# Attention outputs as half-width products, two groups in one run, in a kernel of gated linear attention and two mixtures of experts

## The chip, the cores and the metric

The kernel runs on one core of a Trainium2 chip. The metric is the device time of one execution in microseconds (us). The instruction streams that matter here are TensorE (PE; its weight loads are listed apart as PEld), VectorE (DVE), ScalarE (ACT), GpSimd (POOL) and SyncE (SP), whose queue issues nearly all DMAs of the part of the program that is changed. Each engine works through its own instructions in the order in which the program has them, and waits on semaphores where an instruction needs something of another engine or of a DMA.

## The reference

Three layers follow one another. The first is a linear attention with a decaying state, for 2 batches, 8 heads, 768 tokens and 48 features a head; the outputs of the 8 heads side by side are the 384 features of 1536 tokens. The second is a dense mixture of 4 experts (384 to 1024 to 384), the third a mixture of 8 experts of which each token takes two.

```python
for t in range(S):                                   # attention, per batch and head
    state = alpha[:, :, t, :, None] * state + np.einsum('bhd,bhe->bhde', k[:, :, t], v[:, :, t])
    y[:, :, t] = np.einsum('bhd,bhde->bhe', q[:, :, t], state)

p = domain_probs / (domain_probs.sum(-1, keepdims=True) + 1e-09)      # first mixture
for e in range(E):
    out += p[:, e:e + 1] * (np.maximum(x @ w1[e], 0.0) @ w2[e])

noisy_logits = x @ w_gate + np.log1p(np.exp(x @ w_noise)) * noise     # second mixture, top 2 of 8
```

## The kernel before, in words

**Units.** The 1536 tokens go through the attention in seven units u0 to u6 of 128, 256, 256, 128, 256, 256 and 256 tokens. Heads are worked in pairs: pair p holds head 2p on partitions 0 to 47 and head 2p+1 on partitions 64 to 111. A group is two blocks of (pair, 128-token chunk): a 128-token unit has two groups (pairs 0 and 1, then 2 and 3), a 256-token unit four (one pair with its two chunks each).

**Steps of a group.** `reversed_`, `decays`, `keys`, `queries` transpose alpha, k and q on TensorE (L301) and scale them on VectorE; `scores` (L374) makes the products of keys and queries, with the two heads of a pair on the two halves of TensorE's rows; `keys_back` (L359) transposes the scaled keys, ScalarE copies them to `Kn` (L361); `states` (L397) adds the chunk to the state `St` (VectorE, L404 to L413). `outputs` (L417) makes y: for each block one product of the state with the queries (L427, "inter"), and for each head of the pair one product of v with the masked scores (L430, "intra"), all into the same 96 rows of PSUM. For L430 the v of a head is padded with 48 zero columns, so that both heads of the pair have 96 columns and add into the same rows.

**x, the input of the first mixture.** The mixture's first layer contracts 384 features as three slices `kd` of 128 rows. Pairs 0 to 2 are rows 0 to 95 of the slices; the 96 features of pair 3 are cut in three and fill rows 96 to 127 of each. ScalarE rounds y into `xh` (L451), VectorE writes the rest into `xl` (L455); for pair 3 these are three pieces of 32 rows. For u0 the pieces go to `x32` as plain copies (L446, L448; the profile names the tile `acc`, in whose space it lies). The weights `w1` of experts 0 to 3 are loaded in the same row order, in two DMAs for each quarter (96 and 32 rows, L126).

**What sets the order.** `plan` puts the steps of each group into numbered steps by two tables, NEAR (first three groups) and FAR (the others: `outputs` at +9 in even and +7 in odd groups, a new group every 3 steps). `drive` interleaves them with the first mixture's expert 0, which runs in phases of tokens: 128 (u0), 256 (u1), 384 (u2 and u3), and 256 three times (u4 to u6). A phase starts when the last unit of its tokens is done. In a phase `hidden` makes the first layer (L548 for the first 128 tokens; L552 to L554 otherwise: three products for each `kd`), `product` the second (L572 to L574). What `outputs` leaves to VectorE (`low`) is put into `later` and is issued at the end of its step. DMAs stand in SP's queue in the order in which the program comes to them: the first ones by the list in L649, the others where a step calls `load_unit`. `busy(n)` issues products of ones whose result nothing reads.

**Start.** Before u0 there is `busy(7)` (L197, L200); then alpha, k, q of u0 are transposed as they land.

## Time and profile before

| | us |
|---|---|
| median of 3 runs (lowest, highest) | 743.19 (743.07, 743.55) |
| the profiled execution, its own time | 742.35 |
| span of its trace | 740.4 |
| TensorE busy in the span | 730.3 |
| VectorE, ScalarE, GpSimd busy | 355.6, 244.8, 164.2 |

The profiled execution is 0.84 us below the median; 1.95 us of its time lie outside the span. The attention ends near 166 us of the span; everything that the diff touches lies before that, except the split of the weight loads of experts 1 to 3. TensorE is busy in nearly the whole span, so the view to start from is the one of engines by stretch, and then the places where TensorE stands still or is short of work: the first 40 us.

### The profile page before, as it was taken

The numbers are of one execution on the slowest core, as the hardware profiler recorded it, in microseconds if no ns is written. First come the engines' busy times: TensorE is split into PE (matmuls) and PEld (weight loads), VectorE is DVE, ScalarE is ACT, GpSimd is POOL, SyncE is SP. The second block draws the span as 40 slices with busy tenths as digits, with TensorE's granted clock in tenths as the row PEclk, the third lists the DMA queues.
The fourth block names the chain that finished last, engine by engine and source line by source line (L and its number), as shares of the span: only waits on it lengthen the run. The fifth ranks groups of instructions, "written<-read, shape, count | busy, mean of one in ns | idle before, by whom it ended". The sixth has DMA issues, their size and how long they took to land.

```text
span 740.4 us, 11896 instructions
## 1 busy us (share of the span) xinstructions
PE 730.3 (99%) x4598; PEld 695.7 (94%) x4598; DVE 355.6 (48%) x863; ACT 244.8 (33%) x483; POOL 164.2 (22%) x180
## 2 busy tenths in 40 slices
PE   8999999999999999999999999999999999999996
PEld 6999999999898998989899999999999999999996
DVE  6887667743312222221222525557854464664651
ACT  2543223224302122120413412424544354454340
POOL 3610000005300022000324100012251624524331
PEclk9999999999999999999999999999999999999999
DMA  9985220002700022000123100012754555555620
GB/s 193 204 192 96 40 48 1 1 1 87 196 22 1 0 86 64 23 0 1 44 86 125 35 33 12 22 44 79 246 175 138 180 163 162 188 182 157 192 64 32
DMA packets 98381, 66.96 MB, mean 90 GB/s; under 512 B 57961, under 2 KB 94884, under 8 KB 98320
## 3 DMA queue, kind: packets, MB, share of 16 engines
q1 hardware_dynamic: 93296, 52.02, 26.2%
q0 software_dynamic: 5024, 14.13, 6.0%
q8 instruction: 38, 0.62, 0.3%
q14 instruction: 23, 0.19, 0.1%
HBM read 56.69 MB, written 9.82 MB: 90 GB/s over the span
## 4 chain that ended last, share of the span: by engine, by line
PE 93%; DVE 5%; ACT 1%; issue 0%; POOL 0%; POOLq 0%; DVEq 0%
PE g L552 13%; PE g L553 13%; PE g L554 13%; PE g L572 11%; PE g L573 10%; PE g L574 10%; PE g L1090 3%; PE g L1091 3%; PE g L1092 3%; PE g L430 3%; PE tr L301 2%; PE sc L374 1%; PE tr L1024 1%; PE g L427 1%; PE sc L749 1%; PE sc L397 1%
## 5 line engine op out<-in xcount | busy, mean ns | idle before, releaser
L557 ACT ACTIVATE hh<-g 128x384 fp32r<-128x384 f32 (+8 forms) x200 | 96.8, 484 | 265.2 <-PE g L554 263.6
L561 DVE SCALAR_TENSOR_TENSOR hl<-g,hh 128x384 fp32r<-128x384 f32 (+8 forms) x200 | 109.4, 549 | 144.7 <-ACT hh L557 141.9
L572 PE MATMUL g<-w2h,hl 128*128 128x384 f32 x464 | 161.4, 348 | 0.0
L573 PE MATMUL g<-w2l,hh 128*128 128x384 f32 x464 | 156.1, 336 | 0.0
L574 PE MATMUL g<-w2h,hh 128*128 128x384 f32 x464 | 156.1, 336 | 0.0
L552 PE MATMUL g<-xh,w1l 128*128 128x512 f32 (+2 forms) x360 | 125.8, 349 | 0.0
L554 PE MATMUL g<-xh,w1h 128*128 128x512 f32 (+2 forms) x360 | 123.2, 342 | 0.0
L553 PE MATMUL g<-xl,w1h 128*128 128x512 f32 (+2 forms) x360 | 123.2, 342 | 0.0
L572 PEld LDWEIGHTS g<-w2h,hl 128*128 128x128 f32 x464 | 87.3, 188 | 0.5
L573 PEld LDWEIGHTS g<-w2l,hh 128*128 128x128 f32 x464 | 87.5, 188 | 0.3
L150 POOL TENSOR_TENSOR w1l<-raw,w1h 128x768 fp32r<-128x768 f32 x16 | 29.4, 1852 | 260.8 <-ACT w1h L149 260.8
L574 PEld LDWEIGHTS g<-w2h,hh 128*128 128x128 f32 x464 | 87.2, 188 | 0.0
L605 DVE SCALAR_TENSOR_TENSOR acc<-g,prob,acc 128x384 f32<-128x384 f32 x36 | 22.2, 618 | 116.6 <-PE g L574 116.6
L554 PEld LDWEIGHTS g<-xh,w1h 128*128 128x128 f32 x360 | 67.6, 188 | 5.8
L552 PE MATMUL g<-xth,w1l 128*128 128x256 f32 (+6 forms) x216 | 73.0, 338 | 0.0
L553 PEld LDWEIGHTS g<-xl,w1h 128*128 128x128 f32 x360 | 67.8, 188 | 5.5
L552 PEld LDWEIGHTS g<-xh,w1l 128*128 128x128 f32 x360 | 67.7, 188 | 5.4
L553 PE MATMUL g<-xtl,w1h 128*128 128x256 f32 (+6 forms) x216 | 71.0, 329 | 0.0
L554 PE MATMUL g<-xth,w1h 128*128 128x256 f32 (+6 forms) x216 | 71.0, 329 | 0.0
L149 ACT ACTIVATE w2h<-raw 128x768 fp32r<-128x768 f32 x44 | 37.0, 845 | 36.1 <-issue 23.0
L1042 POOL DMA_INDIRECT out_dram<-yo,si_c x26 | 26.1, 1004 | 87.6 <-DVE yo L1041 81.1
L1090 PE MATMUL g<-hh,w2l 128*128 128x432 f32 (+4 forms) x120 | 43.3, 361 | 0.0
(211 smaller groups left out, 1036.2 us busy)
## 6 DMA issues: line engine op xcount, KB each, us to landing
raw<-in_moe_w_dram SPq DMA_DIRECT2D x76, 384.0 KB, 3.3
raw<-in_moe_w_dram SPq DMA_DIRECT2D x16, 288.0 KB, 3.8
x_a<-in_alpha_dram SPq DMA_DIRECT2D x24, 96.0 KB, 2.8
out_dram<-zero SPq DMA_DIRECT2D x1, 2304.0 KB, 10.9
x2d<-acc SPq DMA_DIRECT2D x12, 192.0 KB, 1.9
x_k<-in_k_dram SPq DMA_DIRECT2D x22, 96.0 KB, 3.0
x_q<-in_q_dram SPq DMA_DIRECT2D x22, 96.0 KB, 2.8
v<-in_v_dram SPq DMA_DIRECT2D x10, 192.0 KB, 3.2
```

The costliest lines, as they stand in the source:

```text
L149: nc.scalar.activation(hi, r, AF.Copy)
L150: (nc.gpsimd if e < E1 or own else nc.vector).tensor_sub(lo, r, hi.bitcast(F32))
L552: nc.tensor.matmul(t[:, :n], wl, hx[:, kd, t0:t0 + n], start=(kd == 0), stop=False)
L553: nc.tensor.matmul(t[:, :n], wh, lx[:, kd, t0:t0 + n], start=False, stop=False)
L554: nc.tensor.matmul(t[:, :n], wh, hx[:, kd, t0:t0 + n], start=False, stop=(kd == KD - 1))
L557: nc.scalar.activation(hh[:, :n], t[:, :n], AF.Relu)
L561: nc.vector.scalar_tensor_tensor(hl[:, :n], t[:, :n], 0.0, hh.bitcast(F32)[:, :n], op0=OP.max, op1=OP.subtract)
L572: nc.tensor.matmul(t[:m, :DM], hl[:, o:o + m], wh, start=(f == 0), stop=False)
L573: nc.tensor.matmul(t[:m, :DM], hh[:, o:o + m], wl, start=False, stop=False)
L574: nc.tensor.matmul(t[:m, :DM], hh[:, o:o + m], wh, start=False, stop=(f == KF - 1))
L1042: nc.gpsimd.indirect_dma_start(out=parts_of_out[s], out_offset=bass.IndirectOffsetOnAxis(ap=SLOT[e * SB + s][2][:n, e * SB + s:e * SB + s ...
L1090: nc.tensor.matmul(t[:, :n], wl, hh[:, :n], start=(f == 0), stop=False)
```

## The change

Parts of it, in the order of the program:

- The weights `w1` of experts 0 to 3 come in four DMAs a quarter (48, 16, 48, 16 rows) instead of two: 64 instead of 32 issues, 8 of the 32 new ones in the list of the start.
- `busy(5)` instead of `busy(7)`.
- v is held with 16 zero columns behind the 48 of each head, the state with 128 columns instead of 96.
- Groups come with pairs 2 and 3 first, then 0 and 1, and the loads of u0 and u1 follow that.
- The intra products become halves: 64 columns of weights each, head 2p into rows 0 to 63 of PSUM, head 2p+1 into rows 64 to 127, on the two halves of TensorE's columns (`halves`, L427 of the changed kernel). The inter product (L458 there) has 128 columns.
- `outputs` does nothing for even groups and both groups at the odd one: first the four inter products, then the eight halves, in one PSUM bank. In u1 to u6 this makes 11 runs out of 22.
- u0 has a function of its own (`first_outputs`): ten halves instead of eight products; ScalarE then copies six pieces of 32 rows and two of 48, VectorE two of 48.
- Of x, heads 2p lie on rows 0 to 47 and 2p+1 on 64 to 111 of slice p; the features of pair 3 fill rows 48 to 63 and 112 to 127. Pair 3 of u1 to u6 is written to a tile `tail` by ScalarE and VectorE, and six DMAs from SBUF to SBUF (16 rows each, both `xh` and `xl`) put it there; they are issued by SP, at the end of the step, after VectorE's part. In a 256-token unit ScalarE and VectorE have four pieces each (two of 128 rows, two of 48) instead of six (three of 96 rows, three of 32).

```diff
@@ -121,12 +121,16 @@
                 r = wpool.tile([P, KD * FG * P], F32, tag="raw", name="raw", bufs=4)
             if t == 1:
                 n = FG * P
-                parts = ((0, P),) if e >= E1 else ((0, 2 * D), (2 * D, P))
-                for p0, p1 in parts:
-                    nc.sync.dma_start(
-                        r.rearrange("p (c f) -> p c f", c=KD)[p0:p1],
-                        w[KD * p0:KD * p1, g * n:(g + 1) * n].rearrange("(c p) f -> p c f", c=KD),
-                    )
+                to = r.rearrange("p (c f) -> p c f", c=KD)
+                cols = slice(g * n, (g + 1) * n)
+                if e >= E1:
+                    nc.sync.dma_start(to, w[:, cols].rearrange("(c p) f -> p c f", c=KD))
+                else:
+                    for j in range(2):
+                        o = (2 * KD + j) * D
+                        nc.sync.dma_start(to[64 * j:64 * j + D],
+                                          w[:2 * D * KD, cols].rearrange("(c j q) f -> j q c f", c=KD, j=2)[j])
+                        nc.sync.dma_start(to[64 * j + D:64 * j + 64], w[o:o + D, cols].rearrange("(c q) f -> q c f", c=KD))
             else:
                 nc.sync.dma_start(
                     r.rearrange("p (c f) -> p c f", c=FG),
@@ -197,7 +201,7 @@
-    busy(7)
+    busy(5)
@@ -228,7 +232,7 @@
-    V = [apool.tile([P, BM, H, 2, D], F32, name=f"v{i}") for i in range(2)]
+    V = [apool.tile([P, BM, H, 64], F32, name=f"v{i}") for i in range(2)]
@@ -257,7 +261,7 @@
-    St = apool.tile([P, HP, BM + 1, 2 * D], F32, name="S")
+    St = apool.tile([P, HP, BM + 1, P], F32, name="S")
@@ -267,18 +271,18 @@
-    xh = xpool.tile([P, KD, N], F32R, name="xh")
-    xl = xpool.tile([P, KD, N], F32R, name="xl")
+    xx = xpool.tile([P, 2, KD, N], F32R, name="xx")
+    xh, xl = xx[:, 0], xx[:, 1]
@@ -286,7 +290,7 @@
-        groups = [[(g * BM // UB + i // UB, i % UB) for i in range(BM)] for g in range(HP * UB // BM)]
+        groups = [[((g * BM // UB + i // UB + 2) % HP, i % UB) for i in range(BM)] for g in range(HP * UB // BM)]
@@ -395,64 +399,92 @@
...
+        def halves(t, todo, opened):
+            v = V[u % 2].rearrange("x c h d -> x c (h d)")
+            for i, (M, p, c, by) in enumerate(todo):
+                for j in range(2):
+                    o = 64 * (2 * p + j) - by
+                    nc.tensor.matmul(t[64 * j:64 * j + 64, at(i)], v[:, c, o:o + 64], M[j], start=not opened and i == 0,
+                                     stop=i == len(todo) - 1)
+
+        def first_outputs(g):
+            t = ps("g", 4)
+            todo = [([st[g, j][:, i, :] for j in range(2)], p, c, 16 if p == KD else 0)
+                    for i, (p, c) in enumerate(groups[g])]
+            if g == 0:
+                todo.append(todo[-1][:3] + (0,))
+            halves(t, todo, False)
+            if g:
+                for r, copy in ((slice(0, D), nc.scalar.copy), (slice(64, 64 + D), nc.vector.tensor_copy)):
+                    copy(x32[r, :BM], t[r, :UM].rearrange("x (c i) -> x c i", c=BM))
+                return
+            for d, (b, i) in enumerate(((0, 1), (0, 2), (1, 1))):
+                for j in range(2):
+                    nc.scalar.copy(x32[64 * j + 32:64 * j + 64, d], t[64 * j + 32 * b:64 * j + 32 * b + 32, at(i)])
+            nc.scalar.copy(x32[:D, KD - 1], t[:D, at(0)])
+            nc.vector.tensor_copy(x32[64:64 + D, KD - 1], t[64:64 + D, at(0)])
+
         def outputs(g):
-            Q = st[g, "Q"]
-            both = ps("g", 4)
-            of = {p: both for p, _ in groups[g]}
-            if u == 0 and g:
-                of[KD] = ps("g", 4)
-            for i, (p, c) in sorted(enumerate(groups[g]), reverse=u == 0 and g > 0):
-                y = of[p][:2 * D, at(i)]
-                inter = not (first and c == 0)
-                if inter:
-                    nc.tensor.matmul(y, St[:, p, slot(c), :], Q[:, at(i)], start=True, stop=False)
-                two = V[u % 2][:, c].rearrange("x h k d -> x (h k d)")
-                for j in range(2):
-                    nc.tensor.matmul(y, two[:, (4 * p + j) * D:(4 * p + j + 2) * D], st[g, j][:, i, :],
-                                     start=not inter and j == 0, stop=j == 1)
-            n = UM if UB == BM else P
+            if u == 0:
+                first_outputs(g)
+                return
+            if g % 2 == 0:
+                return
+            t = ps("g", 4)
+            todo = [(h, i, p, c) for h in (g - 1, g) for i, (p, c) in enumerate(groups[h])]
+            opened = False
+            for k, (h, i, p, c) in enumerate(todo):
+                if not (first and c == 0):
+                    nc.tensor.matmul(t[:, at(k)], St[:, p, slot(c), :], st[h, "Q"][:, at(i)], start=not opened, stop=False)
+                    opened = True
+            halves(t, [([st[h, j][:, i, :] for j in range(2)], p, c, 0) for h, i, p, c in todo], opened)
+            n = UB * P
+            to = slice(starts[u], starts[u] + n)
             pieces = []
-            for i in range(0, BM, n // P):
-                p, c = groups[g][i]
-                to = slice(starts[u] + c * P, starts[u] + c * P + n)
-                y = of[p][:, i * P:i * P + n]
-                if p < KD:
-                    pieces.append((y[:2 * D], slice(0, 2 * D), p, to))
+            tail = None
+            for o in range(0, 2 * UM, 2 * n):
+                y = t[:, o:o + 2 * n].rearrange("x (p i) -> x p i", p=2)
+                if todo[o // P][2]:
+                    tail = apool.tile([P, 2, UM], F32R, tag="tail", name="tail")
+                    pieces.append((y[:, 0], xh[:, KD - 1, to], xl[:, KD - 1, to]))
+                    pieces.append((y[:, 1], tail[:, 0, :n], tail[:, 1, :n]))
                 else:
+                    for j in range(2):
+                        r = slice(64 * j, 64 * j + D)
+                        pieces.append((y[r], xh[r, :2, to], xl[r, :2, to]))
+
+            for y, hi, _ in pieces:
+                nc.scalar.activation(hi, y, AF.Copy)
+
+            def low():
+                for y, hi, lo in pieces:
+                    nc.vector.tensor_sub(lo, y, hi.bitcast(F32))
+                if tail is None:
+                    return
+                for o in range(0, P, 64):
                     for d in range(KD):
-                        pieces.append((y[(P - 2 * D) * d:(P - 2 * D) * (d + 1)], slice(2 * D, P), d, to))
-            if u == 0:
-                for y, r, d, to in sorted(pieces, key=lambda z: z[1].start < 2 * D):
-                    if g and r.start < 2 * D:
-                        nc.vector.tensor_copy(x32[r, d], y)
-                    else:
-                        nc.scalar.activation(x32[r, d], y, AF.Copy)
-                return
-            for y, r, d, to in pieces:
-                nc.scalar.activation(xh[r, d, to], y, AF.Copy)
-
-            def low():
-                for y, r, d, to in pieces:
-                    nc.vector.tensor_sub(xl[r, d, to], y, xh.bitcast(F32)[r, d, to])
+                        nc.sync.dma_start(xx.bitcast(F32)[o + D:o + 64, :, d, to],
+                                          tail.bitcast(F32)[o + 16 * d:o + 16 * d + 16, :, :n])
 
             later.append(low)
 
@@ -644,7 +676,7 @@
-        load_unit(0, "akq", i * HP // 2, (i + 1) * HP // 2)
+        load_unit(0, "akq", (1 - i) * HP // 2, (2 - i) * HP // 2)
@@ -652,7 +684,7 @@
-            load_unit(1, what[0], int(what[1]) * HP // 2, (int(what[1]) + 1) * HP // 2)
+            load_unit(1, what[0], (1 - int(what[1])) * HP // 2, (2 - int(what[1])) * HP // 2)
```

TensorE's order around the first outputs of u1 (`_100`, `_102`: buffers of the unit; `Kn` the copied keys; `x2` two in a row). Before:

```order
L427 MATMUL g<-Q,S 96x128
L430 MATMUL g<-M,v_106 96x128 x2
L427 MATMUL g<-Q,S 96x128
L430 MATMUL g<-M,v_106 96x128 x2
L397 MATMUL sc_494<-v_106,Kn 128x96 x2
L359 MATMUL tr<-ident,K 128x128 x2
L301 MATMUL tr<-ident,x_a_100 128x128 x2
L427 MATMUL g<-Q,S 96x128
L430 MATMUL g<-M,v_106 96x128 x2
L427 MATMUL g<-Q,S 96x128
L430 MATMUL g<-M,v_106 96x128 x2
L301 MATMUL tr<-ident,x_k_102 128x128 x2
```

The same place in the changed kernel:

```order
L401 MATMUL sc_496<-v_104,Kn 128x96 x2
L363 MATMUL tr<-ident,K 128x128 x2
L305 MATMUL tr<-ident,x_a_98 128x128 x2
L458 MATMUL g<-Q,S 128x128 x4
L427 MATMUL g<-M,v_104 64x128 x8
L305 MATMUL tr<-ident,x_k_100 128x128 x2
```

The outputs of the even group no longer stand ahead of the state's products; both groups' outputs are one run behind the transposes.

SP's queue around the outputs of u3 (a 128-token unit; the loads are those of u5). Before:

```order
L250 DMA x_a_99<-in_alpha_dram 128x4x48 x2
L248 DMA v_106<-in_v_dram 128x8x48 x2
L250 DMA x_k_101<-in_k_dram 128x4x48 x2
L250 DMA x_q_103<-in_q_dram 128x4x48 x2
L250 DMA x_a_99<-in_alpha_dram 128x4x48 x2
```

The same place in the changed kernel:

```order
L254 DMA x_a_97<-in_alpha_dram 128x4x48 x2
L252 DMA v_104<-in_v_dram 128x8x48 x2
L486 DMA xx<-tail 16x2x128 x6
L254 DMA x_k_99<-in_k_dram 128x4x48 x2
L254 DMA x_q_101<-in_q_dram 128x4x48 x2
```

The six loads into the gaps of x stand behind the two loads of v.

VectorE's order at the outputs of u0 (`acc` here is `x32`, the rest are steps of u1's first group). Before:

```order
L317 SCALAR_TENSOR_TENSOR suffix_109<-tr,tri 128x127 x2
L324 SCALAR_TENSOR_TENSOR A<-tr,tri 128x128 x2
L325 RECIPROCAL rc<-A 128x2
L446 COPY acc<-g 96x128
L329 TENSOR_TENSOR K<-tr,suffix_109 128x256
```

The same place in the changed kernel:

```order
L321 SCALAR_TENSOR_TENSOR suffix_107<-tr,tri 128x127 x2
L445 COPY acc<-g 48x128
L328 SCALAR_TENSOR_TENSOR A<-tr,tri 128x128 x2
L329 RECIPROCAL rc<-A 128x2
L439 COPY acc<-g 48x256
L333 TENSOR_TENSOR K<-tr,suffix_107 128x256
```

There are two copies instead of one, the first of them ahead of the scans of `A`; the built program makes that first copy wait for ScalarE's copies of the same PSUM bank.

## Rows read from the trace of the kernel before

**Rows 1.** The page: busy times, and the chain that ended last by engine.

```profile
PE 730.3 (99%) x4598; PEld 695.7 (94%) x4598; DVE 355.6 (48%) x863; ACT 244.8 (33%) x483; POOL 164.2 (22%) x180
PE 93%; DVE 5%; ACT 1%; issue 0%; POOL 0%; POOLq 0%; DVEq 0%
```

**Rows 2.** Stretches: us, busy time (and instructions) of each engine, PEclk, DMA share, GB/s.

```profile
0.00:20.00 20.00, 17.25 (x124) 13.03 (x125) 13.75 (x49) 6.20 (x18) 5.94 (x24) 1.00 0.94 194
20.00:40.00 20.00, 19.80 (x175) 18.91 (x172) 17.06 (x57) 12.40 (x31) 13.79 (x9) 1.00 0.94 206
80.00:180.00 100.00, 100.00 (x793) 97.62 (x792) 61.83 (x172) 31.36 (x82) 5.66 (x4) 1.00 0.08 19
```

**Rows 3.** Timeline, TensorE, outputs in u3: start, us, line, tiles, records.

```profile
68.48 0.38 PE L427 MATMUL g<-Q,S 128*96 128x128 f32 x2
68.70 0.60 PE L430 MATMUL g<-M,v 128*96 128x128 f32 x4
69.13 0.38 PE L359 MATMUL tr<-ident,K 128*128 128x128 f32 x2
```

**Rows 4.** Timeline, TensorE, a run of scores on two halves of the rows.

```profile
29.93 0.34 PE L573 MATMUL g<-w2l,hh 128*128 128x384 f32 x1
30.11 0.34 PE L574 MATMUL g<-w2h,hh 128*128 128x384 f32 x1
30.37 1.16 PE L374 MATMUL sc<-Q,G 48*128 48x128 f32 x16
31.47 0.44 PE L301 MATMUL tr<-ident,x_k 128*128 128x128 f32 x2
```

**Rows 5.** Timeline, first outputs of u1 and the state behind them, VectorE and TensorE.

```profile
24.53 1.13 DVE L413 SCALAR_TENSOR_TENSOR S<-S,A,sc 48x48 f32<-48x48 f32 x4
25.41 0.46 PE L427 MATMUL g<-Q,S 128*96 128x128 f32 x2
```

**Rows 6.** Timeline, TensorE, the start.

```profile
1.14 3.17 PE L197 MATMUL g<-ones_b 128*128 128x512 bf16 x7 [1.14 <-DVE ones_b L192]
4.10 0.61 PE L301 MATMUL tr<-ident,x_a 128*128 128x128 f32 x2
10.27 1.91 PE L430 MATMUL g<-M,v 128*96 128x128 f32 x16
12.47 0.83 PE L548 MATMUL g<-acc,raw 128*128 128x128 f32 x6
```

**Rows 7.** Timeline, ScalarE and VectorE, copies of u0's outputs and their neighbours.

```profile
11.34 1.31 ACT L448 ACTIVATE acc<-g 96x128 f32<-96x128 f32 x5 [9.24 <-PE g L430]
11.41 0.71 DVE L324 TENSOR_TENSOR_SCAN A<-tr,tri 128x128 f32<-128x128 f32 x2
12.24 0.27 DVE L446 COPY acc<-g 96x128 f32<-96x128 f32 x1
```

**Rows 8.** Timeline, SP's queue: start of the issue, us, line, tile, number.

```profile
5.79 1.20 SPq L126 DMA_DIRECT2D raw<-in_moe_w_dram  x2
21.32 2.70 SPq L131 DMA_DIRECT2D acc<-in_moe_w_dram  x2
36.10 0.45 SPq L250 DMA_DIRECT2D x_a<-in_alpha_dram  x1
```

**Rows 9.** Timeline, TensorE, first products of the phase of u1.

```profile
39.48 0.28 PE L552 MATMUL g<-xh,w1l 128*128 128x256 f32 x1
```

**Rows 10.** Timeline, end of u3's outputs: TensorE, ScalarE and SP.

```profile
71.49 0.60 PE L430 MATMUL g<-M,v 128*96 128x128 f32 x4
74.92 0.34 PE L552 MATMUL g<-xh,w1l 128*128 128x384 f32 x1
72.13 1.14 ACT L451 ACTIVATE xh<-g 96x128 fp32r<-96x128 f32 x4 [2.08 <-PE g L430]
72.12 1.69 SPq L248 DMA_DIRECT2D v<-in_v_dram  x2
73.90 1.08 SPq L250 DMA_DIRECT2D x_k<-in_k_dram  x2
```

**Rows 11.** The page, DMA issues: KB each, median us from issue to landing.

```profile
x2d<-acc SPq DMA_DIRECT2D x12, 192.0 KB, 1.9
x_k<-in_k_dram SPq DMA_DIRECT2D x22, 96.0 KB, 3.0
```

More of the change, by code (lines that the diff above doesn't have):

```diff
@@ L247, in load_unit @@
                 if nm == "v":
-                    nc.sync.dma_start(V[u % 2][:, c, hs, 0], frm)
+                    nc.sync.dma_start(V[u % 2][:, c, hs, :D], frm)
                     continue
@@ L269 @@
         filled(t, 1.0)
-    filled(V[0][:, :, :, 1, :], 0.0)
+    filled(V[0][:, :, :, D:], 0.0)
     filled(X["a", 1][:, :, :, D:], 1.0)
@@ L275 @@
         filled(St[:, p], 0.0)
-    filled(V[1][:, :, :, 1, :], 0.0)
+    filled(V[1][:, :, :, D:], 0.0)
     for nm in "kq":
         filled(X[nm, 0][:, :, :, D:], 0.0)
-    xh = xpool.tile([P, KD, N], F32R, name="xh")
-    xl = xpool.tile([P, KD, N], F32R, name="xl")
+    xx = xpool.tile([P, 2, KD, N], F32R, name="xx")
+    xh, xl = xx[:, 0], xx[:, 1]
     def attention(u):
@@ L397, in states @@
                 nc.tensor.matmul(t[:, i * 2 * D:(i + 1) * 2 * D].rearrange("x (j d) -> x j d", j=2), Kn[:, i, :],
-                                 V[u % 2][:, c, 2 * p:2 * p + 2, 0, :], start=True, stop=True)
+                                 V[u % 2][:, c, 2 * p:2 * p + 2, :D], start=True, stop=True)
             for j in range(2):
@@ L401, in states @@
                 cols = slice(j * D, (j + 1) * D)
+                here = slice(64 * j, 64 * j + D)
                 if first and UB == 1:
                     p0 = groups[g][0][0]
-                    nc.vector.tensor_copy(St[rows, p0:p0 + BM, slot(1), cols],
+                    nc.vector.tensor_copy(St[rows, p0:p0 + BM, slot(1), here],
                                           t[rows, :BM * 2 * D].rearrange("x (i d) -> x i d", i=BM)[:, :, cols])
@@ L408, in states @@
                     o = t[rows, i * 2 * D + j * D:i * 2 * D + (j + 1) * D]
-                    to = St[rows, p, slot(c + 1), cols]
+                    to = St[rows, p, slot(c + 1), here]
                     if first and c == 0:
@@ L412, in states @@
                     else:
[L413 removed]
+                        nc.vector.scalar_tensor_tensor(to, St[rows, p, slot(c), here],
                                                        A[rows, i * P + P - 1:i * P + P], o,
                                                        op0=OP.mult, op1=OP.add)
[L417 to L455 removed]
```

1 line of the change is left out of this document (removed).

## The prediction

> **What bounds the kernel now.** I read the page's busy times and its chain first. TensorE is busy 99% of the span, and 93% of the chain that ended last is TensorE's own work [rows 1]; so what shortens TensorE's stream shortens the kernel, and what makes TensorE wait lengthens it, wherever no slack is left. The view by stretch then says where there is slack: from 80 to 180 us TensorE is busy 100.00 of 100 us, in the first 20 us 17.25 and in the next 20 us 19.80 [rows 2]. The first 40 us are also the place where the DMA share is 0.94, against 0.08 after 80 us, and where VectorE is busy 17 of 20 us. The granted clock is 1.00 in all these stretches, so rows from anywhere can be compared, except the very start: seven products of 512 columns from 1.14 to 4.10 us are 0.42 us each [rows 6], 512 columns in 0.42 us, which is the lower of the two levels, 1.2 GHz.
>
> So the change has one steady gain (TensorE's outputs, 11 runs up to 166 us) and its prices lie at two kinds of places: the start, and the moments at which a phase of the mixture begins and x has only just been made.
>
> **Halves of the columns.** The four records of L430 in u3 start at 68.70 and the next instruction starts at 69.13 [rows 3]: 0.109 us for each. Two groups have eight intra products, two records each: 16 x 0.109 = 1.74 us. With halves there are as many records, but two at a time if the two column halves work side by side. No row shows column halves. The nearest one is the run of scores, also 16 records, on two halves of the rows: the slot of the product ahead of it ends at 30.11 + 0.18 = 30.29 (L573 to L574 is 0.18), the next instruction starts at 31.47, so the run takes 1.18 us [rows 4]. That is 0.87 (eight pairs at 0.109) and 0.31 for going into the divided array and out of it. The gain of a run is then 1.74 - 1.18 = 0.56 us. Bounds: 0.87 if the switch costs nothing, and a loss of 0.31 if the halves run one after the other and the switch is paid all the same. I take 0.56, from the row that is nearest.
>
> The Trainium skill, "TensorEngine Tiling (Array Packing)", section Key Properties, says that a change of the tiling mode drains the engine and that tiles work independently. The 0.31 us agree with the drain; by the page the gain of a run would be the same 0.56, since the change pays one switch in and out for eight halves.
>
> The inter product grows from 96 to 128 columns. Two of its records take 0.22 us (68.48 to 68.70) [rows 3] and the two records ahead of the run of outputs have the same price at 128 columns of weights, so that is nothing; the bound is 0 to 0.2 us for all of them.
>
> Merging two groups also takes the even group's outputs away from where they stood: between the scores and the state's products. In u1 this was cover. The inter product of the second chunk starts at 25.41 while VectorE's four state updates run from 24.53 to 25.66 [rows 5]: TensorE got there no earlier than the state did. Without 1.3 us of outputs ahead (two times 0.22 + 0.43 [rows 3]) it gets to the same wait earlier and stands there longer, and the gain of that run goes into the wait. The second run of u2 stands likewise close behind its own state's products. I count both as 0 (between a gain of 0.56 and a loss of 0.75 each, which is the lost cover less the gain). Nine runs are left: 9 x 0.56 = **-5.0 us** (bounds -7.8 and +2.8).
>
> **The start.** Two of seven unread products go: 2 x 0.42 = 0.85 us earlier [rows 6], and the first transposes do wait for these products, as alpha has landed by then. What follows on VectorE and TensorE keeps that, up to the outputs of u0. There it is lost. Before, ScalarE makes five copies from 11.34 (1.31 us, 0.26 each), VectorE one at 12.24 that takes 0.27, and the first product of the mixture starts at 12.47 [rows 6, 7]. In the changed kernel VectorE's first copy waits for ScalarE's first seven: from about 10.4 (11.34 - 0.85, a little less for the shorter run) seven times 0.26 is 12.2; then the copy, 0.27, the scans of A, 0.71, a reciprocal of about 0.1, and the second copy of twice the width, some 0.4: 13.65. That is 1.2 us after 12.47, and on TensorE the transposes of alpha and the state's products of u1 are queued behind the mixture's product, so that VectorE's own chain, which is what this stretch waits for, moves along. I take **+1.2 us**. It could come down to 0, where waits that are there anyway take it up (TensorE idles 2.75 us in the first 20 [rows 2], 1.14 of them ahead of its first product).
>
> SP's queue gets eight issues more in this stretch. A pair of issues of w1 took 1.20 us [rows 8], so the eight are some 4.2 to 4.8 us of issue. But the bytes are the same and the DMA share is 0.94 [rows 2]: the queue waits for the engines. Two loads of w2 took 2.70 us of issue instead of some 1.1 [rows 8], and such slack takes the added issues up. I count nothing beside the 1.2, with an upper bound of 1.1 us more for loads that land late. Cover: the start's own shift.
>
> **The six loads into the gaps, u1.** The tail of u1 comes with its first run, near 26 us, and is not needed until 39.48 [rows 9]. But SP's queue has loads of u2 and u3 ahead of it, the last being the one issued at 36.10 for 0.45 us [rows 8]. So the six issues begin near 36.6, plus what the start's added issues leave, up to 1 us. At some 0.5 us each, the fourth begins at 38.1 and the sixth at 39.1; loads took 1.9 to 3.0 us to land [rows 11], so these two land at 40.0 to 41.1 and 41.0 to 42.1. The first slice needs the first and the fourth, the third slice the third and the sixth. The mixture's product would start at 39.48 + 1.2 = 40.7, its third slice 0.7 later. **+0.5 us**, between 0 and 1.8.
>
> **The six loads, u3.** Here all four pairs come in one run that ends where the last L430 records ended, near 71.9, and the phase of 384 tokens starts at 74.92 [rows 10]: 3 us for ScalarE, VectorE, SP and the DMAs. ScalarE and VectorE need about 1.3 us, up to 73.2 (before: 1.14 for four pieces on ScalarE [rows 10]). SP first issues the two loads of v, which wait for the same outputs: 72.12 to 73.81 [rows 10]. The six issues then begin at 73.8, the fourth at 75.3, and with 1.9 us to land [rows 11] it is there at 77.2: TensorE waits 2.3 us. The sixth lands at 78.2, just in time for the third slice. Before, x of u3 was written by ScalarE and VectorE alone. **+2.3 us**; 1.0 if an issue takes 0.35 us and the second v goes out faster, 3.4 at 3.0 us to land. Behind the six stand the loads of k and q of u5 (73.90 before [rows 10]), 3 us later and used tens of us later: nothing.
>
> **What costs nothing.** The tails of u2 and u4 to u6 come with the first run of four groups, some 13 us ahead of the need as in u1, and after 80 us the DMA share is 0.08 [rows 2]. The 24 further issues of w1 lie in the same quiet queue. ScalarE and VectorE lose pieces (six become four), but neither is the bound there (61.83 and 31.36 of 100 us [rows 2]).
>
> **Sum.** -5.0 + 1.2 + 0.5 + 2.3 = -1.0 us, against the profiled execution of 742.35: 741.35. The median of the runs is 0.84 above that execution, so as a median 742.2.
>
> **The rivals.**
> *Waits that don't come.* The queue of the start takes up more (start +0.6), u1's loads are in time and u3's wait is at its low bound of 1.0: -5.0 + 0.6 + 1.0 = -3.4, 739.8. For it: the largest wait rests on issue times that I have only for larger loads. Against it: the two v's ahead in the queue are plain in the order.
> *Slower, by the loads in SBUF.* At u3 the loads land after 3.0 us instead of 1.9 (wait 3.4), at u1 the queue is a full issue burden later (1.8), and the start keeps 2.0: -5.0 + 2.0 + 1.8 + 3.4 = +2.2, 745.4. It decides from 6.5 us of added waits in all (5.0 and 1.5). For it: six issues in a row on one queue, each waited for; against it: the DMA engines are half free at 72 us.
> *The halves don't run side by side.* Then each run loses 0.31 instead of gaining 0.56: nine times 0.87 more, +7.8, 750.0. For it: no row has column halves, and both halves stream all 128 rows, where the scores' halves stream 64 each. Against it: the weights' loads and products of the scores do overlap on one array [rows 4]. The Trainium skill's page "TensorEngine Tiling (Array Packing)", section Restrictions and Gotchas (Feature Incompatibilities), speaks for it a little: column tiling excludes the fast weight load, so a half's weights might arrive late; no row here shows that.
>
> **How the numbers follow.** My forecast 0.42 (its own range 740.5 to 743.8), waits that don't come 0.33, slower by the loads 0.14, halves in sequence 0.11. A measurement of this kernel can tell about 0.2%, 1.5 us, from no change. Faster: all of the second and 0.05 of the first, 0.38; within 0.2%: 0.37 of the first and 0.03 of the third, 0.40; slower: 0.11 and 0.11, 0.22. The range leaves out the halves in sequence and the ends of the others: 738.6 to 746.8.
>
> **What would show it.** TensorE's timeline: in each run of u2 to u6 eight pairs of half records 0.109 apart, the run 1.2 us long; records singly at 0.109 would be the third rival. TensorE's waits: one of some 2.3 us ahead of the first 128x384 product near 75 us with a DMA as releaser, one of half a us near 41, and the first product of the mixture at 13.6 instead of 12.5. No wait at 75 us would make the prediction too slow by 2.3; a wait at the first product of a later phase would make it too fast.

## The result, and the profile after

The changed kernel takes 749.38 us (median of 4 runs, 747.82 to 750.35) against 743.13 us of the kernel before; the ratio is 1.0081, with a 95% interval of 1.0061 to 1.0102. It is slower by 6.2 us, and the time lies outside the forecast range of 738.6 to 746.8. The profiled execution took 750.12 us, its span is 748.3 us against 740.4; it is one of the two longer ones of the four (750.12 and 750.35; the others 747.82 and 748.64), so its waits may be longer than those of the other two.

The page after: TensorE's busy time hardly differs from [rows 1] (728.4 against 730.3 us), but the chain that ended last is TensorE's for 87% only, and SP's queue and DMAs have a part in it.

```profile
PE 728.4 (97%) x4600; PEld 687.1 (92%) x4600; DVE 354.4 (47%) x852; ACT 242.6 (32%) x474; POOL 164.3 (22%) x180
PE 87%; DVE 6%; SPq 2%; ACT 1%; DMA 1%; issue 1%; POOL 0%; POOLq 0%; DVEq 0%
```

By stretch (columns as in [rows 2]): TensorE loses 1.8 us of busy time in the first 20 us, 0.8 in the next and 4.1 from 80 to 180 us, where it was busy 100.00 of 100 us before. From 40 to 60 us it is busy 17.37 of 20, where it was busy throughout before:

```profile
40.00:60.00 20.00, 20.00 (x185) 19.34 (x185) 16.83 (x52) 7.25 (x21) 1.84 (x1) 1.00 0.79 166
```

The four stretches after:

```profile
0.00:20.00 20.00, 15.48 (x107) 10.42 (x108) 13.17 (x45) 6.27 (x19) 5.42 (x24) 1.00 0.74 168
20.00:40.00 20.00, 19.01 (x174) 16.90 (x174) 16.86 (x56) 11.06 (x27) 12.74 (x9) 1.00 0.91 197
40.00:60.00 20.00, 17.37 (x161) 15.89 (x159) 15.37 (x45) 8.19 (x21) 2.99 (x2) 1.00 0.67 151
80.00:180.00 100.00, 95.91 (x761) 90.93 (x761) 61.67 (x168) 26.95 (x71) 0.00 (x0) 0.98 0.12 24
```

TensorE's waits (engine, line, releaser: us in total, times, longest) say what stands there. L584 is the first product of a mixture's phase, L458 the inter product, L580 the mixture's product of the first 128 tokens; the 1.8 us put down to "issue" lie at the start, at 13.23:

```profile
PE g L584 <- DMA xx<-tail: 5.6, 3, 3.2
PE tr L305 <- issue: 1.8, 1, 1.8
PE g L458 <- DVE S L418: 1.3, 2, 0.7
PE g L580 <- DMA raw<-in_moe_w_dram: 0.7, 1, 0.7
```

To see where the time came, I compare the start of the same product of the first mixture in the two traces. The difference only moves where something of the attention, or a wait, lies between. These are differences in us to the kernel before, worked out from TensorE's records; the columns are the kernels of the experiments below, of which the three in the middle leave pair 3 of u1 to u6 out of x:

| product that starts before at | after | no loads in SBUF | and copies on ScalarE | groups apart | both places mended |
|---|---|---|---|---|---|
| 12.5 (first of the mixture) | +1.9 | +2.3 | +1.0 | +1.1 | +0.6 |
| 40.5 (behind u1) | +5.3 | +3.1 | +2.4 | +1.5 | +2.2 |
| 61.4 (amid u2 and u3) | +5.0 | +3.1 | +2.4 | +1.5 | +2.3 |
| 79.4 (behind u3) | +10.0 | +3.1 | +2.3 | +1.2 | +3.6 |
| 111.1 (behind u4) | +8.9 | +1.9 | +1.2 | +0.8 | +2.4 |
| 140.5 (behind u5) | +8.1 | +1.1 | +0.4 | +0.3 | +1.6 |
| 171.2 (behind u6) | +8.2 | +1.2 | +0.5 | -0.2 | +1.7 |

So the change loses 1.9 us at the start, 3.4 in u1 and 5.0 at u3; u4 and u5 give 1.1 and 0.8 back. From 171 us to the end nothing more happens that matters (+7.8 at the last product).

**The halves do run side by side.** TensorE's timeline of one run of u1, in which nothing waits: four inter products in 0.98 us, eight halves in 1.02 us, to be compared with [rows 3].

```profile
37.78 1.05 PE L458 MATMUL g<-Q,S 128*128 128x128 f32 x8
38.76 1.09 PE L427 MATMUL g<-M,v 128*64 128x128 f32 x16
39.78 0.44 PE L305 MATMUL tr<-ident,x_k 128*128 128x128 f32 x2
```

16 records in 1.02 us are eight pairs at 0.109 and 0.15 more; the two halves of a pair start 0.006 us apart. The eight inter records ahead take 0.98 us instead of the 0.88 of eight slots of 0.11 (a slot runs from one start to the next), so that the switch costs some 0.25 in all, against the 0.31 that the prediction took from the scores. Together 2.00 us against 4 x (0.22 + 0.43) = 2.60 before: 0.60 a run.

**u1.** SP's queue comes to the six loads at 39.91, and they are issued over 3.98 us; the first slice of x needs the first and the fourth of them. The phase starts at 44.23, after a wait of 2.30 us, where [rows 9] had 39.48.

```profile
39.36 0.45 SPq L254 DMA_DIRECT2D x_a<-in_alpha_dram  x1
39.91 3.98 SPq L486 DMA_DIRECT2D xx<-tail  x6
44.23 0.36 PE L584 MATMUL g<-xx,w1l 128*128 128x256 f32 x1 [2.30 <-DMA xx<-tail]
```

**u3.** The run of outputs ends at 76.83. VectorE writes its part of the tail at 78.41 only, SP issues the two loads of v until 79.16 and then the six; the phase starts at 83.22, after 3.19 us of waiting, where without a wait it would have followed the product ahead of it at 79.88.

```profile
75.81 1.09 PE L427 MATMUL g<-M,v 128*64 128x128 f32 x16
78.41 0.29 DVE L481 TENSOR_TENSOR tail<-g,tail 128x128 fp32r<-128x128 f32 x1
76.94 2.22 SPq L252 DMA_DIRECT2D v<-in_v_dram  x2
79.26 3.78 SPq L486 DMA_DIRECT2D xx<-tail  x6
83.22 0.41 PE L584 MATMUL g<-xx,w1l 128*128 128x384 f32 x1 [3.19 <-DMA xx<-tail]
```

Behind that wait the granted clock falls. The first six products still start 0.17 us apart; then come stretches of 0.60 and 0.55, and products of 384 columns start 0.32 us apart instead of 0.175, which is the lower level, 1.2 GHz. Eleven of them cost 1.6 us more.

```profile
84.00:86.00 2.00, 2.00 (x8) 1.88 (x8) 0.00 (x0) 0.30 (x1) 0.00 (x0) 0.60 0.67 124
86.00:88.00 2.00, 2.00 (x8) 2.00 (x8) 0.56 (x1) 0.19 (x1) 0.00 (x0) 0.55 0.38 72
85.14 0.52 PE L586 MATMUL g<-xx,w1h 128*128 128x384 f32 x1
```

**The start.** VectorE's first copy waits 1.72 us for ScalarE's seven and starts at 12.61, its second is at 13.89, and the mixture's first product follows at 14.37 ([rows 6, 7] before: 12.24 and 12.47).

```profile
12.61 0.29 DVE L445 COPY acc<-g 48x128 f32<-48x128 f32 x1 [1.72 <-ACT acc L444]
13.89 0.43 DVE L439 COPY acc<-g 48x256 f32<-48x256 f32 x1
14.37 0.94 PE L580 MATMUL g<-acc,raw 128*128 128x128 f32 x6 [0.74 <-DMA raw<-in_moe_w_dram]
```

The wait is put down to a load of `w1`, which is the event that came last by the profile; VectorE's copy ends at 14.32 and fits as well. The trace of a kernel with the same start (v behind the six loads, below) names the copy:

```profile
PE g L580 <- DVE acc L439: 0.7, 1, 0.7
```

### The profile page after: what moved, and what is told of

Read it like the earlier page. It is cut to its first block, busy times and chain, and to the rows that moved or that the text cites. A ratio compares the mean times of both kernels' runs of the same rounds, so it can differ in the third digit from the quotient of the medians.

```text
span 748.3 us, 11999 instructions
## 1 busy us (share of the span) xinstructions
PE 728.4 (97%) x4600; PEld 687.1 (92%) x4600; DVE 354.4 (47%) x852; ACT 242.6 (32%) x474; POOL 164.3 (22%) x180
## 4 chain that ended last, share of the span: by engine, by line
PE 87%; DVE 6%; SPq 2%; ACT 1%; DMA 1%; issue 1%; POOL 0%; POOLq 0%; DVEq 0%
PE g L584 13%; PE g L585 12%; PE g L586 12%; PE g L604 10%; PE g L606 10%; PE g L605 10%; PE g L1122 3%; PE g L1123 3%; PE g L1124 3%; PE tr L305 2%; PE tr L1056 1%; PE g L427 1%; DVE hl L593 1%; PE sc L781 1%; PE g L458 1%; PE tr L1144 1%
## 5 line engine op out<-in xcount | busy, mean ns | idle before, releaser
L584 PE MATMUL g<-xx,w1l 128*128 128x512 f32 (+2 forms) x360 | 127.0, 353 | 5.6 <-DMA xx<-tail 5.6
L585 PE MATMUL g<-xx,w1h 128*128 128x512 f32 (+2 forms) x360 | 123.7, 344 | 0.3 <-DVE xx L481 0.3
L586 PE MATMUL g<-xx,w1h 128*128 128x512 f32 (+2 forms) x360 | 123.7, 344 | 0.0
L584 PEld LDWEIGHTS g<-xx,w1l 128*128 128x128 f32 x360 | 68.2, 189 | 12.1 <-issue 6.4
L585 PEld LDWEIGHTS g<-xx,w1h 128*128 128x128 f32 x360 | 68.3, 190 | 6.0 <-DVE xx L481 0.6
L586 PEld LDWEIGHTS g<-xx,w1h 128*128 128x128 f32 x360 | 68.1, 189 | 5.8
L584 PE MATMUL g<-xth,w1l 128*128 128x256 f32 (+6 forms) x216 | 73.0, 338 | 0.0
```

Source lines behind the costliest of these rows:

```text
L584: nc.tensor.matmul(t[:, :n], wl, hx[:, kd, t0:t0 + n], start=(kd == 0), stop=False)
L585: nc.tensor.matmul(t[:, :n], wh, lx[:, kd, t0:t0 + n], start=False, stop=False)
L586: nc.tensor.matmul(t[:, :n], wh, hx[:, kd, t0:t0 + n], start=False, stop=(kd == KD - 1))
```

## The experiments

My theory after the two traces: the loads from SBUF to SBUF, queued on SP, make two phases late, and the rest is the start. The rival: the outputs themselves lose, since their inter products now wait for the state. Medians of the kernel before beside these runs were 742.8 to 743.0.

**Without the loads in SBUF.**

```diff
-                        r = slice(64 * j, 64 * j + D)
+                        r = slice(64 * j, 64 * j + 64)
...
-                if tail is None:
-                    return
-                for o in range(0, P, 64):
-                    for d in range(KD):
-                        nc.sync.dma_start(xx.bitcast(F32)[o + D:o + 64, :, d, to],
-                                          tail.bitcast(F32)[o + 16 * d:o + 16 * d + 16, :, :n])
```

> The changed kernel without its 36 loads from SBUF to SBUF: the features of pair 3 of units u1 to u6 are left out of x (zeros stand in the gaps), all else is the same. Theory (the loads queue on SP and land late): the waits of 2.3 and 0.2 us near 44 us and of 3.2 us near 83 us go, and with the second one the 1.6 us of lower clock behind it; 749.4 - 2.5 - 4.8 = about 742. Rival (the time went into the outputs themselves, whose inter products wait 3.0 us for the state in four runs): the two waits go, but other things are as late, and it stays above 746.

743.33 us, ratio 1.0004 (0.9995 to 1.0014). The two waits and the lower clock are gone: 6 of the 6.2 us hang on these loads. The rival, over 746, is out. It is still 1.3 us above what I expected: from the first product to 171 us only 1.1 us are won (+2.3 to +1.2 in the table), and nothing of it in u1 to u3. The waits of 3.0 us in four runs, on which I had built the rival, were a misreading: that sum has each wait twice, once for the weight load and once for the product. There are two waits, with TensorE idle for 1.3 us.

**v behind the six loads.**

```diff
-                load_unit(u + 2, "v")
+                later.append(lambda: load_unit(u + 2, "v"))
```

> The changed kernel with the loads of v (for the unit after next) issued behind the six loads into the gaps instead of ahead of them. Theory (SP's order): at the outputs of u3 the six issues start 2.2 us earlier, the wait of 3.2 us ahead of the first 384-column product falls to about 1, and the lower clock behind it goes too: -2.2 to -3.8, so 745.6 to 747.2; u1 unchanged. Rival (the loads are slow by themselves, six writes into 16 partitions each): the wait stays near 3, 749.

747.99 us, ratio 1.0077 (1.0056 to 1.0097). The six start 1.9 us after the run's end instead of 2.4, since they now wait for VectorE; the wait falls from 3.2 to 2.75 us only, and the clock falls all the same.

```profile
77.12 3.79 SPq L486 DMA_DIRECT2D xx<-tail  x6
81.14 0.66 PE L584 MATMUL g<-xx,w1l 128*128 128x384 f32 x1 [2.75 <-DMA xx<-tail]
```

The theory was wrong here in what is next late: VectorE's part of the tail, ready at 78.70 after, was only some 0.5 us ahead of the end of v's issues. Then four issues of 0.63 us and a landing of about 2 us make the chain. (Up to u1 the program is the changed kernel's, but in this execution SP came to the six of u1 at 38.37 and not at 39.91, and u1's waits were 1.3 us instead of 2.5, which is why u3 is to be read from the trace and not from the total.)

**u0's copies on ScalarE alone.**

```diff
-            nc.vector.tensor_copy(x32[64:64 + D, KD - 1], t[64:64 + D, at(0)])
+            nc.scalar.copy(x32[64:64 + D, KD - 1], t[64:64 + D, at(0)])
```

(and the same for the second group's)

> The changed kernel with VectorE's two copies of the outputs of u0 given to ScalarE, so that VectorE's scans are not behind ScalarE's seven copies. Theory: the first product of the mixture starts near 13.6 instead of 14.4, but what starts u1's phase is SP's queue (the six loads begin at 39.9), so the 0.8 us are given back in a longer wait near 44: 749, no change beyond 0.5. Rival (the start's delay passes through to the end): -0.8, 748.6, and the wait near 44 stays at 2.3.

749.52 us, the same as the changed kernel. The mixture starts 0.7 us earlier than after (+1.2 instead of +1.9), and the lead has gone by the end of u2 (+4.8 against +5.0). But it did not go in the theory's way:

```profile
38.17 3.98 SPq L486 DMA_DIRECT2D xx<-tail  x6
42.50 0.36 PE L584 MATMUL g<-xx,w1l 128*128 128x256 f32 x1 [1.54 <-DMA xx<-tail]
44.00:46.00 2.00, 2.00 (x11) 2.00 (x11) 0.92 (x3) 0.77 (x2) 0.00 (x0) 0.50 0.83 191
82.81 0.42 PE L584 MATMUL g<-xx,w1l 128*128 128x384 f32 x1 [2.96 <-DMA xx<-tail]
84.00:86.00 2.00, 2.00 (x13) 2.00 (x13) 0.56 (x1) 0.49 (x1) 0.00 (x0) 1.00 0.88 164
```

In this execution SP came to the six of u1 at 38.17, the wait was shorter and not longer, and what was won went to the lower clock behind it: products of 256 columns started 0.21 us apart instead of 0.117, 1.4 us in all. At u3 the wait was 2.96 us and the clock stayed at 1.00. So it is not shown that a load takes up the start's delay; four executions of each kernel, spread over 2.5 us and more, leave it open.

**Both.**

> Both together: no loads into the gaps (pair 3 of u1 to u6 left out of x) and u0's copies on ScalarE alone. Theory: without the late loads the start's delay does count, so this is 0.5 to 1 us below the version without the loads alone, about 741.2. Rival (the start's delay is absorbed elsewhere): the same as without the loads, about 742.

742.75 us, ratio 0.9997 (0.9988 to 1.0007), 0.6 below the version without the loads alone. The intervals overlap, but the traces agree: the first product comes 1.35 us earlier, and 0.7 of that is left at 171 us (+0.5 against +1.2). Without late loads about half of what the start wins comes through.

This trace also shows where the gain of the outputs goes. Only two of the eleven runs stand for the state, u1's first and u2's second, the two that the prediction had counted as 0; the other nine take 2.01 us as above, or 1.56 in u4, where half of the inter products fall away.

```profile
26.41 0.49 PE L458 MATMUL g<-Q,S 128*128 128x128 f32 x2 [0.36 <-DVE S L418]
62.19 0.49 PE L458 MATMUL g<-Q,S 128*128 128x128 f32 x2 [0.58 <-DVE S L418]
```

Counted from start to start between the first product and 171 us, with waits taken out, the intra products take 8.3 us less than before and the inter products 1.6 more: -6.7, 0.61 for each of the eleven runs. What eats it up is elsewhere: 3.3 us more of waits of 0.15 us and longer (of them 0.9 for the state, 0.8 for VectorE's part of x at the start of two phases, the rest ahead of transposes, for VectorE, ScalarE and a load), 2.4 us in longer slots of the transposes, and 0.5 in other products. So only 0.5 us of 6.7 comes through. Why the transposes' slots grew is not shown.

**Groups apart again.** From here to the run with seven unread products the base is the last kernel.

```diff
-            if g % 2 == 0:
-                return
...
-            todo = [(h, i, p, c) for h in (g - 1, g) for i, (p, c) in enumerate(groups[h])]
+            todo = [(h, i, p, c) for h in (g,) for i, (p, c) in enumerate(groups[h])]
```

> Like the version without loads into the gaps and with u0's copies on ScalarE (pair 3 of u1 to u6 left out of x), but each group has its own outputs at its old place, still as halves. Theory (merging two groups took away cover: six of the eleven merged runs gain nothing or lose): the waits of the inter products for the state go, the runs of u1, u2 and u3 no longer lose, but each group pays its own switch, so 22 times 0.87 - 0.75 = 2.6 us of gain against the measured net 2.4 of the merged runs: 742.5. Rival (the merged runs' missing gain has nothing to do with their place): eleven more switches of 0.3 us, 746.

742.29 us, ratio 0.9994 (0.9984 to 1.0004). As the theory has it, the form without merging is no slower, though its premise was wrong: two of the merged runs, and not six, had failed to gain. In the table u1 costs 0.4 us with groups apart and 1.4 merged, while u4 gives 0.4 instead of 1.2. Merging saves switches and brings more waits: 3.3 us more than before when merged, 1.2 apart. The waits of the inter products got shorter but didn't vanish (0.7 us in the same two places, 0.9 merged). The pair is not quite clean, as the kernel with groups apart also drops pair 3's pieces for ScalarE and VectorE, which the merged one still writes.

**Merged runs one step later.**

```diff
-           {"reversed": 0, "decays": 0, "keys": 1, "queries": 2, "keys_back": 3, "scores": 4, "states": 6, "outputs": 7})
+           {"reversed": 0, "decays": 0, "keys": 1, "queries": 2, "keys_back": 3, "scores": 4, "states": 6, "outputs": 8})
...
-            rows_at[u] = end + 2
+            rows_at[u] = end + (1 if u else 2)
```

> The same version with the merged runs one step of the side stream later (pair 3 of u1 to u6 left out of x). Theory (place): the state is there when the inter products come, and the runs of u1, u2, u3, u5 and u6 that gained nothing gain 0.3 to 0.56 us each: about 1.5 us less, 741.2. Rival (the work ahead is what is short, and the wait passes to the next instruction): no change, 742.75.

754.12 us, ratio 1.0156 (1.0138 to 1.0174): 11 us slower than its base. The inter products wait no longer, but the transposes of k, now ahead of u1's first run, do, for 3.1 us (they take the PSUM buffer that VectorE's scans still read), and in all five phases the second product, the first to read VectorE's part of x, waits for it.

```profile
PE g L579 <- DVE xx L481: 6.0, 5, 1.4
PE tr L305 <- DVE A L328: 3.1, 1, 3.1
```

The rival's mechanism holds, the wait passes on; its number does not, since the waits became longer and not equal. This place had no slack.

**Seven unread products.**

> The same version with seven unread products at the start instead of five (pair 3 of u1 to u6 left out of x). Theory (u0's chain hangs on its first transposes): 0.85 us later from the start to the end, 743.6. Rival (something else sets the start, loads or copies): 742.75, no change.

743.16 us, ratio 1.0002 (0.9993 to 1.0012), 0.4 above its base. The first product of the mixture is 0.95 us later, at 171 us 0.4 are left. Neither theory: half of it is absorbed.

**All causes taken away, first form.** v behind, pair 3's pieces first, slices outer, and

```diff
+                        (nc.scalar if UB == 1 and o else nc.sync).dma_start(
...
+                if u == 1 and "tail" not in st:
+                    held.append(lambda: load_unit(v, names, p1 - 2, p1))
```

> The changed kernel, complete, with the causes found so far taken away: u0's copies on ScalarE and in two fewer pieces, the loads of u3's inputs behind u1's six loads into the gaps, for u3 half of the six on ScalarE's queue and v behind them, pair 3's pieces first. Theory: no wait near 41 us, one of about 0.5 us near 78, no lower clock: 742.5 to 743.3. Rival (loads into 16 partitions are late wherever they are issued): one or both waits of over 1.5 us stay, 745 or more.

753.18 us, ratio 1.0131 (1.0111 to 1.0151). At u1 the theory holds: the six loads start at 36.27, and the wait is gone (+2.43 at the product of 40.5 us). At u3 a load on ScalarE's queue stopped SP's:

```profile
68.48 9.68 SPq L254 DMA_DIRECT2D x_a<-in_alpha_dram  x2
78.25 1.10 SPq L252 DMA_DIRECT2D v<-in_v_dram  x2
81.59 1.49 PE L401 MATMUL sc<-v,Kn 128*128 128x96 f32 x4 [5.61 <-DMA v<-in_v_dram]
SPq L254 <- DMA xx<-tail: 8.8, 1, 8.8
```

Two issues took 9.68 us instead of 1.01, v came late and TensorE waited 5.61 us; a further wait of 1.04 us for the tail and a granted clock of 0.50 from 82 to 90 us make up most of the rest. The last line, of SP's own waits, names the cause: the second of the two issues waited 8.8 us for a load of the tail, though its target has nothing to do with it. In the trace's records the loads of SP and ScalarE signal by the same eight semaphores in turn; this issue and ScalarE's first load have the same one, the latter landed at 77.77, and the issue begins at 77.78.

**The two places mended.** As before, but with all loads on SP, v at its old place in the queue, and u3 without loads in SBUF: pair 3 is computed a second time, shifted by 16 columns, and written in pieces of 32 rows.

```diff
+            for t, blocks in ((ps("g", 4), [(KD, 16), (KD, 0)]), (ps("g", 4), [(p, 0) for p in range(KD)])):
+                for k, (p, by) in enumerate(blocks):
+                    h, i = by_pair[p]
+                    o = (p * (BM + 1) + slot(0)) * P - by
+                    nc.tensor.matmul(t[:, at(k)], S_[:, o:o + P], st[h, "Q"][:, at(i)], start=k == 0, stop=False)
```

> The changed kernel, complete, without the two late places: u1's six loads stand in SP's queue ahead of the loads of u3's inputs (slice by slice); u3 has no loads in SBUF, its pair 3 is computed once more shifted by 16 columns and written by ScalarE and VectorE in pieces of 32 rows as in u0; u0's copies on ScalarE in two fewer pieces. Theory (the two places and the start are all that was lost): like the version without loads into the gaps, 742.3 to 743.3, with no wait over 0.8 us near 41 or 78. Rival (the loads of the other units, or u3's added products and pieces, cost as much): 745 or more.

743.45 us, ratio 1.0007 (0.9998 to 1.0015). Complete, and 5.9 us below the changed kernel, which is the two places and the start's copies together: at u3 only the second product waits, 0.32 us, for VectorE's last pieces.

```profile
77.91 0.34 PE L624 MATMUL g<-xx,w1l 128*128 128x384 f32 x1
78.56 0.45 PE L625 MATMUL g<-xx,w1h 128*128 128x384 f32 x1 [0.32 <-DVE xx L473]
```

**The same, groups apart.**

> The same, with each group's outputs at its old place in the 256-token units (u3 stays merged). Theory (merging costs cover what it saves in switches): 0 to 0.6 us below the merged one, 742 to 743. Rival (one run for two groups is the better form once nothing is late): 0.5 or more above it.

743.86 us, ratio 1.0011 (1.0002 to 1.0020). Not told apart from the merged one; here the form with groups apart has the more pieces, six in a 256-token unit instead of four.

**The kernel before with five unread products.**

> The kernel before with five unread products instead of seven, nothing else. Theory (from the pair of runs with five and seven, which differ by 0.4): -0.3 to -0.4, 742.4. Rival (the first transposes set the pace of the whole start): -0.85, 741.9. Second rival (the start waits for loads and copies anyway): 742.8, no change.

742.82 us, ratio 1.0008 (0.9996 to 1.0021): no change. The mixture starts 0.83 us earlier, and at 27 us nothing is left, because the transposes of k wait longer for ScalarE, 0.84 us instead of 0.20, and start at the same time (before, then this run):

```profile
26.51 0.44 PE L301 MATMUL tr<-ident,x_k 128*128 128x128 f32 x2 [0.20 <-ACT Kn L361]
26.54 0.44 PE L301 MATMUL tr<-ident,x_k 128*128 128x128 f32 x2 [0.84 <-ACT Kn L361]
```

**Only u1's loads moved forward.**

> The changed kernel, complete, with one thing moved: the loads of u3's inputs stand behind u1's six loads into the gaps in SP's queue (and in all units the six go slice by slice, pair 3's piece first). Theory (two separate places, 2.8 us at u1 and the rest at u3): the wait near 44 us goes; at u3 two issues fewer stand ahead of the first slice, but the two loads of v still do, and its wait stays above 2 us with lower clock behind it: 746 to 747. Rival (what is won at u1 is lost again at u3, whose queue is as long): 749.

747.72 us, ratio 1.0064 (1.0052 to 1.0077). u1's wait is gone, u3's is 3.03 us with the lower clock behind it. The total is 1.7 us below the changed kernel while u1's two waits had been 2.5; at u3 it loses 4.9 us in this trace. So u1 and u3 are two places, and u3 is the larger.

No version beats the kernel before: the best, 742.29 us, leaves out part of x, and of the complete ones the two with both places mended are level with it or 0.1% above, the others 0.6% and more.

## Why the prediction was wrong

In the trace after, at 171 us, the terms of the sum are +1.9 for the start, +2.5 for the waits at u1, +4.8 for the wait at u3 with its lower clock, and -1.0 for all that is left, the outputs above all: +8.2. Forecast were +1.2, +0.5, +2.3 and -5.0. So two steps failed by about as much: **the loads in SBUF**, 4.5 us too low, and **that the runs' gain of 5.0 us comes through**, 4.0 us too high.

- **What bounds the kernel.** Half right: the losses lie in the first 90 us. But "what shortens TensorE's stream shortens the kernel" failed where I had seen no wait, after 80 us too: u6's two runs bring nothing.
- **The halves.** The mechanism, the size of a run and the count of nine were right: 0.60 measured, 0.56 forecast, the two runs set aside are the ones that wait, and the third rival (halves in sequence) is out. The Trainium skill, "TensorEngine Tiling (Array Packing)", section Key Properties, says that tiles work independently; for column halves this trace agrees, with two halves 0.006 us apart. The Trainium skill, "TensorEngine Tiling (Array Packing)", section Restrictions and Gotchas (Feature Incompatibilities), says that column tiling excludes the fast weight load; that cost nothing here, as the pairs start 0.109 us apart, but no row shows whether there was a fast load to lose. The step that failed is **-5.0 us at the end**. Without late loads u4 and u5 give 1.2 and 0.8 us, u2, u3 and u6 nothing, and u1 loses 1.4 (fourth column of the table): -0.5 in all. The prediction put VectorE and ScalarE under what costs nothing, because they are busy for 62 and 31 of 100 us; but TensorE, being earlier, met new waits for them, 3.3 us in all with the state, and slots of transposes that are 2.4 us longer. Merging against groups apart makes no measurable difference. No run has the halves in the old layout of x, so what they would bring by themselves stays open.
- **The start, +1.2.** Measured +1.9: the right chain, VectorE behind ScalarE's copies, with each link a little longer (12.61 instead of 12.2 for the first copy). That the start counts in full was wrong: of 1.35 us between two kernels without late loads 0.7 arrives at 171 us, of 0.95 by the unread products 0.4, and in the kernel before 0.83 us of them are nothing by 27 us. Whether in the changed kernel the wait at u1 takes up the start, so that the two terms must not be added, is argued and not shown.
- **u1, +0.5.** Measured 2.5 in the two waits, and 1.3 and 1.7 in the traces of two kernels with the same loads there (v behind the six loads, copies on ScalarE). SP came to the six at 39.91, 38.37 and 38.17, not at 36.6 to 37.6: the eight added issues were taken up by the queue's slack only in part (x of u3: 36.10 before [rows 8], 39.36 after), and an issue took 0.66 us, not 0.5. What the added issues cost at 24 to 29 us, where ScalarE's copies of w2 wait for loads, was not tried alone.
- **u3, +2.3.** The wait was 3.2, near the upper bound of 3.4: v took 2.2 us of issue instead of 1.7, and the issues of the six 0.63 us each instead of 0.5. Even without v ahead the wait is 2.75, as VectorE's part is ready only 1.9 us after the run, where I had put 1.3. What the sum lacked altogether is the lower clock behind the wait, 1.6 us more. No row of before has a wait of that kind; the start of the trace, at the lower clock, would have given a bound for it.
- **The rivals.** The second one, slower by the loads in SBUF, is what happened, with 5.7 us of waits at the two places, 1.6 of lower clock and 1.9 at the start: above the 6.5 us from which it was to decide. I gave it 0.14, and its own 745.4 is 4.0 too low, as it kept the -5.0 of the outputs and had nothing for the clock. Against it I had put that the DMA engines are half free at 72 us; the loads waited for SP and for landing, not for bandwidth (DMA share 0.58 and 0.12 in the two stretches of 2 us from 80 us).

## What to carry to other kernels

A load in SBUF that replaces a copy by an engine has a chain of its own: the queue ahead of it, about 0.65 us an issue and some 2 us to land. Put that chain beside the slack between the last write and the first read, place by place, and count queue positions in the order in which SP stands at that time, not in the one before the change; here that moment moved by 1.5 us between two executions whose program was the same up to there. When the busiest engine gets faster, list the waits that it will meet sooner: of 6.7 us won in the products themselves 0.5 came through here. And when several groups are merged into one run, look at what the removed run stood in front of.

## What was not expected of the hardware

- After 3.2 us without work the granted clock stayed up for 1.1 us of products and then was 0.60 and 0.55 in the next two stretches of 2 us (products of 384 columns 0.32 us apart, 1.2 GHz); after 2.3 us at u1 in the same trace it stayed at 1.00. After 2.75 and 3.03 us in two other kernels it fell. But in the kernel with u0's copies on ScalarE it fell to 0.50 after 1.54 us and stayed at 1.00 after 2.96. So the length of a wait alone does not tell, in these runs, whether the clock falls.
- A run of eight halves with 64 columns takes nearly what the scores take for the same 16 records on halves of the rows: 1.12 us against 1.18 [rows 4], both counted from the end of the slot ahead.
- One load issued from ScalarE held SP's queue for 8.8 us, by a semaphore that the two queues' loads share.
